# A decode layer on one core: the output transfer issued by SyncE behind the closing barrier instead of by ScalarE inside the block

## The chip, the core and the metric

The kernel runs on 1 core of one Trainium2 chip. The metric is the device time of one execution in microseconds (us). The kernel before takes 293.27 us (median of 3 runs, 293.23 to 293.54). Stamps in the text count from the span's start, the first instruction in the profile.

## What is computed

One decode step for two rows (B = 2, one token each): layer norm, attention over a sliding window of a cache, output projection, residual, layer norm, a gated feed-forward block, residual.

```python
W = min(4096, max(256, Sk // 4))          # 2048 of the 8192 cached positions
q = (x @ wq).reshape(B, Sq, Hq, Dh).transpose(0, 2, 1, 3)
k, v = k_cache[:, :, Sk - W:, :], v_cache[:, :, Sk - W:, :]
p = softmax(einsum("bhqd,bhkd->bhqk", q, k) * Dh ** -0.5)
a = einsum("bhqk,bhkd->bhqd", p, v).transpose(0, 2, 1, 3).reshape(B, Sq, Hq * Dh) @ wo

h  = x + A(layernorm(x))                  # A: the attention above
h2 = h + (gelu(n @ w_gate) * (n @ w_up)) @ w_down      # n = layernorm(h)
```

D = 640, 32 heads of 192, F = 1536, all in bfloat16. The output is [2, 1, 640], 2,560 bytes.

## The kernel before

Nearly everything is a stream of loads from HBM, 122.29 MB in all. A ring buffer in SBUF of six slots of 24,576 bytes per partition takes the keys and the values in 16 groups (two rows, four heads to a group), then the weights: wq after the first group of keys, wo in four parts, at the end w_gate, w_up in two pieces and w_down in four (`load`, `pump`, line 347). All loads are issued by SyncE, 44 of them, each when the slot that it overwrites has been read. TensorE transposes the keys (line 555), ScalarE and VectorE copy them out of PSUM, and scores, softmax and the product with the values follow group by group, in a loop of four trips on TensorE.

The program is written as a list of operations in order. `_Prog.op` notes for each the tiles that it reads (R) and writes (W) and the PSUM banks that it touches (X), and from these its dependences. `resolve` turns dependences into waits on semaphores, one for each engine's class of operations and one for each load. `emit` then puts one engine's operations into that engine's own stream, in the order of the list: waits, instruction, increment. Each engine has its own function inside `with nc.Block() as block` (lines 867 to 888). When the block closes, each engine branches out of its function, drains and enters a barrier: it increments one semaphore, GpSimd collects the increments and raises a second one, for which the others wait. In the profile all of this stands at line 867. Instructions written after the block come behind this barrier in the stream of the engine that has them. In the kernel before that is one wait on SyncE (line 890), for the semaphore `dout`.

The end of the computation, in the order of the code: the last two parts of the output projection (line 708), the sum of the hidden row and the second layer norm (lines 773 to 790), the products with w_gate and w_up (line 801) and the gate, with work on VectorE and ScalarE (the last operation on ScalarE is the activation at line 840, which scales the product with w_up), the transposes (line 810), the product with w_down in four pieces (line 850), the copy of the result from PSUM into the tile `yrow` on VectorE (line 856), and the transfer of `yrow` to the output in HBM (line 857), which ScalarE issues. It takes 8 rows of 160 elements, from every 16th partition of `yrow`, and writes them as [2, 4, 160]. ScalarE issues one other transfer, the load of x at the beginning (line 410).

A transfer adds 16 to its semaphore when it is complete. The waits on `dout` and on `yrow`'s writer are what orders the end:

```python
dve(lambda e: e.tensor_copy(yrow[0:113, :], m1[0:113, 0:160]), W=["y"], X=["m1"])
P.op("act", lambda e: e.dma_start(out..., yrow[0:113:16, :]), R=["y"], W=["out"], dma="dout")
...
nc.sync.wait_ge(sems["d", "dout"], 16)
```

Of the kernel before, what the change touches and what calls it, by code (L numbers as in the profile page):

```python
# [227 lines left out]
def bass_sequential_preLN__sliding_block_cached__geglu_ffn__decode_kernel(  # L228
# [12 lines left out]
    with ExitStack() as ctx:  # L241

        def sb(name, shape, dt):
            return ctx.enter_context(nc.sbuf_tensor(name, shape, dt))
# [66 lines left out]
        yrow = sb("yrow", [128, 160], BF16)  # L311
# [14 lines left out]
        P = _Prog()  # L326
# [62 lines left out]
        def dve(fn, R=(), W=(), X=(), cls=1):  # L389
            return P.op("dve", fn, R, W, X, cls=cls)  # L390
# [75 lines left out]
        def _x_T(e):  # L466
# [11 lines left out]
            R=["pi"] + [("bits", k) for k in range(11)], W=["pti"])  # L478
# [262 lines left out]
        for J in range(4):  # L741
# [32 lines left out]
           R=["rs", "bsel"], X=[("t", 3)])  # L774
# [47 lines left out]
        def rjb(t):  # L822
# [18 lines left out]
            W=[("osb", 0), ("osb", 1)], X=["o"])  # L841
        vT = ffn_columns(urow, [("osb", 0), ("osb", 1)], tps[1], 1)
        dve(tt(uT[:, :, 0:17:16].rearrange("p (r j) b -> p r j b", r=4), vT, rjb(ga[:, 0, :]), ALU.mult), R=["ga0"], W=["uT"], X=[("t", 1)])
        for i, (f0, f1) in enumerate(WDC):
            wd, wtoks = where["wd", i]

            def fn(e, f0=f0, f1=f1, wd=wd):
# [6 lines left out]

            pe(fn, R=["uT"] + wtoks, X=["m1"])
        dve(lambda e: e.tensor_copy(yrow[0:113, :], m1[0:113, 0:160]), W=["y"], X=["m1"])  # L856
        P.op("act", lambda e: e.dma_start(out[:, 0, :].rearrange("b (r n) -> r b n", r=4), yrow[0:113:16, :]), R=["y"], W=["out"],
             dma="dout")


        P.resolve({("dve", 0): 4 * 11, ("dve", 1): 8, ("act", 0): 4 * 6, ("pool", 0): 4})
        sems = {}
# [4 lines left out]
        with nc.Block() as block:  # L867

            @block.gpsimd
            def _(e):  # L870
                P.emit("pool", e, sems)

            @block.sync
            def _(e):
                P.emit("sp", e, sems)

            @block.vector
            def _(e):
                P.emit("dve", e, sems)

            @block.scalar
            def _(e):
                P.emit("act", e, sems)

            @block.tensor
            def _(e):
                P.emit_loop(e, sems, 4, ["a0", (0, None, ["oc"]), "a1", (0, 3, ["op"]), "a2", "b0", "b1", "b2", "c0", "c1", "c2",
                                         (None, 3, ["d0", "d1", "d2"])])

        nc.sync.wait_ge(sems["d", "dout"], 16)  # L890


# [26 lines left out]
```

## Time and profile before

| what | value |
|---|---|
| median of 3 runs | 293.27 us (293.23 to 293.54) |
| the profiled execution | 293.36 us |
| its span, first to last instruction | 291.9 us |
| mean granted TensorE clock | 0.849 |
| PE, matmuls | 197.7 us busy (68%) |
| PE, weight loads | 153.8 us (53%) |
| VectorE (DVE) | 128.4 us (44%) |
| ScalarE (ACT) | 96.2 us (33%) |
| GpSimd (POOL) | 8.6 us (3%) |
| queue of SyncE's loads (q1) | 6336 packets, 98.1% of the 16 DMA engines' span |
| queue of ScalarE's transfers (q10) | 16 packets, 0.0% |
| read from HBM | 122.29 MB, 419 GB/s over the span |

The span is shorter than the time of its own execution by 1.44 us (its unrounded value is 291.92): what lies ahead of the first and behind the last instruction of the program. An engine's share is busy time over the span; time in which a sequencer issues a transfer, waits, drains or takes part in a barrier is not counted as busy, and such instructions are named after their queue (ACTq, SPq). The chain that ended last is followed from the last compute instruction backwards; what lies behind that one (the output transfer, the barrier, the last wait) is not in it, and is read from the lines' own views. "Landing" is the last increment that a transfer makes on its semaphore.

### The profile page before, as it was taken

The numbers are of one execution on the slowest core, as the hardware profiler recorded it, in microseconds if no ns is written. First come the engines' busy times: TensorE is split into PE (matmuls) and PEld (weight loads), VectorE is DVE, ScalarE is ACT, GpSimd is POOL, SyncE is SP. The second block draws the span as 40 slices with busy tenths as digits, with TensorE's granted clock in tenths as the row PEclk, the third lists the DMA queues.
The fourth block names the chain that finished last, engine by engine and source line by source line (L and its number), as shares of the span: only waits on it lengthen the run. The fifth ranks groups of instructions, "written<-read, shape, count | busy, mean of one in ns | idle before, by whom it ended". The sixth has DMA issues, their size and how long they took to land.

```text
span 291.9 us, 5066 instructions
## 1 busy us (share of the span) xinstructions
PE 197.7 (68%) x2141; PEld 153.8 (53%) x2141; DVE 128.4 (44%) x311; ACT 96.2 (33%) x120; POOL 8.6 (3%) x36
## 2 busy tenths in 40 slices
PE   2570758858579197849594598658597858585784
PEld 1470445838376194629382585456575656563341
DVE  5960086434336254516264155426267426262231
ACT  2150125533333152616161154325254334251001
POOL 4000020000000000000000000000000000000000
PEclk9997799797959689987979589979689979796557
DMA  7997999999999999999999999999999999999994
GB/s 280 446 506 345 430 431 427 434 427 431 433 430 428 431 431 432 431 431 431 431 409 448 431 431 428 431 428 431 431 431 428 431 431 431 431 431 418 427 412 172
DMA packets 6362, 122.44 MB, mean 419 GB/s; under 512 B 718, under 2 KB 848, under 8 KB 1360
## 3 DMA queue, kind: packets, MB, share of 16 engines
q1 hardware_dynamic: 6336, 122.29, 98.1%
q8 instruction: 7, 0.11, 0.2%
q14 instruction: 3, 0.02, 0.0%
q10 hardware_dynamic: 16, 0.01, 0.0%
HBM read 122.29 MB, written 0.00 MB: 419 GB/s over the span
## 4 chain that ended last, share of the span: by engine, by line
DMA 76%; PE 20%; SPq 2%; DVE 1%; issue 0%
DMA ring<-in_A_k_cache_dram 57%; PE tps L555 16%; DMA ring<-in_A_wq_dram 10%; DMA ring<-in_B_w_down_dram 10%; SPq L347 2%; PE tps L576 2%; PE ops L657 1%; PE m L708 1%; PE m L690 1%; DVE ering L408 0%; PE m L641 0%; PE m L850 0%; DVE ktr L567 0%; PE m L671 0%; DVE yrow L856 0%
## 5 line engine op out<-in xcount | busy, mean ns | idle before, releaser
L555 PE MATMUL tps<-identf,ring 128*128 128x128 f32 x768 | 116.7, 322 | 46.8 <-DMA ring<-in_A_k_cache_dram 45.7
L555 PEld LDWEIGHTS tps<-identf,ring 128*128 128x128 f32 x768 | 107.9, 169 | 49.8 <-DMA ring<-in_A_k_cache_dram 47.1
L564 ACT ACTIVATE ktr<-tps 128x1024 bf16<-128x1024 bf16 x80 | 79.3, 1023 | 87.9 <-PE tps L555 87.9
L567 DVE COPY ktr<-tps 128x1024 bf16<-128x1024 bf16 x112 | 74.1, 688 | 74.9 <-PE tps L555 74.3
L632 ACT ACTIVATE eexp<-sm,nm 128x512 bf16<-128x512 f32 x16 | 11.5, 721 | 63.0 <-DVE nm L630 63.0
L657 PE MATMUL ops<-ring,ering 128*32 128x384 bf16 x512 | 25.0, 339 | 3.5 <-DMA ring<-in_A_v_cache_dram 3.4
L621 DVE CUSTOM_DVE_ANT_1 sm<-sps,mska 128x512 f32<-128x512 f32 x16 | 11.1, 691 | 33.7 <-PE sps L613 33.7
L613 PE MATMUL sps<-ktr,rq 128*16 128x512 bf16 x384 | 24.6, 388 | 1.1 <-POOL rq L408 1.1
L657 PEld LDWEIGHTS ops<-ring,ering 128*32 128x32 bf16 x512 | 12.7, 99 | 12.4 <-DMA ring<-in_A_v_cache_dram 5.4
L613 PEld LDWEIGHTS sps<-ktr,rq 128*16 128x16 bf16 x384 | 9.4, 88 | 11.3 <-POOL rq L408 1.2
L628 PEld LDWEIGHTS m<-mrhs,pm 128*128 128x128 bf16 x16 | 1.5, 96 | 23.4 <-DVE mrhs L404 23.4
L628 PE MATMUL m<-mrhs,pm 128*128 128x16 bf16 x16 | 2.9, 183 | 15.7 <-DVE mrhs L404 15.7
L408 POOL TENSOR_TENSOR rq<-qs,mask 128x96 bf16<-128x96 bf16 x16 | 5.6, 359 | 194.6 <-PE sps L613 161.4
L576 PE MATMUL tps<-ring,xnT 128*32 128x384 bf16 x80 | 5.0, 422 | 9.0 <-DMA ring<-in_A_wq_dram 9.0
L576 PEld LDWEIGHTS tps<-ring,xnT 128*32 128x32 bf16 x80 | 2.8, 121 | 11.0 <-issue 9.2
L408 DVE TENSOR_TENSOR ering<-m,mask 128x256 bf16<-128x256 f32 x16 | 6.7, 420 | 3.3 <-PE m L641 3.3
L599 DVE CAST qs<-ops 128x384 bf16<-128x384 f32 x1 | 0.6, 557 | 14.9 <-PE ops L594 14.9
L708 PE MATMUL m<-ring,ot 128*2 128x320 bf16 x96 | 5.5, 381 | 1.6 <-DMA ring<-in_A_wo_dram 1.6
L788 ACT ACTIVATE lnv<-tps,eps_t 98x1 f32<-98x1 f32 x1 | 0.3, 262 | 17.3 <-PE tps L786 17.3
L641 PE MATMUL m<-sel,eexp 128*128 128x64 bf16 x64 | 5.1, 207 | 1.2 <-ACT eexp L632 1.2
L641 PEld LDWEIGHTS m<-sel,eexp 128*128 128x128 bf16 x64 | 4.8, 112 | 1.7 <-DVE nm L630 1.3
L408 DVE TENSOR_TENSOR orow<-m,wm 128x1536 bf16<-128x1536 f32 x3 | 5.3, 1751 | 0.0
(124 smaller groups left out, 84.7 us busy)
## 6 DMA issues: line engine op xcount, KB each, us to landing
ring<-in_A_k_cache_dram SPq DMA_DIRECT2D x16, 3072.0 KB, 31.7
ring<-in_A_v_cache_dram SPq DMA_DIRECT2D x16, 3072.0 KB, 27.6
ring<-in_A_wq_dram SPq DMA_DIRECT2D x1, 7680.0 KB, 28.2
ring<-in_A_wo_dram SPq DMA_DIRECT2D x4, 1920.0 KB, 21.7
ring<-in_B_w_gate_dram SPq DMA_DIRECT2D x1, 1920.0 KB, 32.4
ring<-in_B_w_up_dram SPq DMA_DIRECT2D x1, 1536.0 KB, 24.7
ring<-in_B_w_down_dram SPq DMA_DIRECT2D x1, 960.0 KB, 27.2
ring<-in_B_w_down_dram SPq DMA_DIRECT2D x1, 480.0 KB, 27.9
```

Of the source, the lines that this page charges most:

```text
L347: P.op("sp", lambda e, v=v, src=src: e.dma_start(v, src), W=toks + [("sem", sem)], dma=sem)
L408: return lambda e: e.tensor_tensor(out=out, in0=a, in1=b, op=op)
L555: ins = e.transpose(tps[bi][:, 128 * u:128 * (u + 1)], kv[:, off:off + 128], identf[:, :])
L564: act(lambda e, dst=dst, bv=bv: e.activation(out=dst, in_=bv, func=ACT.Copy), W=[("kt", n)], X=[("t", bi)])
L567: dve(lambda e, dst=dst, bv=bv: e.tensor_copy(dst, bv), W=[("kt", n)], X=[("t", bi)], cls=0)
L576: ins = e.matmul(tps[0][32 * r:32 * (r + 1), 0:384], lhsT=xnT[:, c, 32 * J:32 * (J + 1)], rhs=wq[:, c, 1536 * J + 384 * r:1536 * J + 384 * ...
L613: ins = e.matmul(sps[32 * ch:32 * ch + 16, :], lhsT=rq[:, g % 4, k, :], rhs=ktr[:, k // 2, 1024 * ch + k % 2:1024 * (ch + 1):2], start=(k ...
L621: dve(lambda e: e.tensor_tensor_reduce(out=sm[:, :].rearrange("p (u x) -> p u x", u=4), in0=sps[:, :].rearrange("p (u x) -> p u x", u=4), ...
L632: act(lambda e: e.activation(out=eexp[:, :], in_=sm[:, :], func=ACT.Exp, bias=nm[:, 0:1], scale=1.0, accum_out=zr[:, g % 4:g % 4 + 1]), R= ...
L641: ins = e.matmul(o, lhsT=eexp[:, 128 * u:128 * (u + 1)], rhs=sel64[:, :], start=True, stop=True)
L657: ins = e.matmul(ops_[32 * r:32 * (r + 1), 0:384], lhsT=ering[:, g % 4, t, :], rhs=vv[:, 384 * t:384 * (t + 1)], start=(g % 4 == 0 and t < 4),
L708: ins = e.matmul(m1[32 * r:32 * r + 2, 192:512], lhsT=ot[:, kk, :], rhs=wo[:, kk - k0, 320 * h:320 * (h + 1)], start=(kk == 1 or J < 2 and ...
```

## The change

The transfer of `yrow` is listed as an operation of SyncE instead of ScalarE and its handle is kept as `last`. SyncE's function in the block emits all of SyncE's operations but this one; it is emitted after the block, ahead of the wait for `dout`. Its dependence on the copy into `yrow` stays, as a wait on VectorE's semaphore in front of it. Source, destination and semaphore are the same. In the streams: ScalarE has one instruction less at its end; SyncE has one more between the closing barrier and its last wait; PE, VectorE and GpSimd have the same instructions in the same order.

```diff
         dve(lambda e: e.tensor_copy(yrow[0:113, :], m1[0:113, 0:160]), W=["y"], X=["m1"])
-        P.op("act", lambda e: e.dma_start(out[:, 0, :].rearrange("b (r n) -> r b n", r=4), yrow[0:113:16, :]), R=["y"], W=["out"],
-             dma="dout")
+        last = P.op("sp", lambda e: e.dma_start(out[:, 0, :].rearrange("b (r n) -> r b n", r=4), yrow[0:113:16, :]), R=["y"], W=["out"],
+                    dma="dout")
...
             @block.sync
             def _(e):
-                P.emit("sp", e, sems)
+                P.emit("sp", e, sems, [o for o in P.per["sp"] if o is not last])
...
+        P.emit("sp", nc.sync, sems, [last])
         nc.sync.wait_ge(sems["d", "dout"], 16)
```

## The prediction

> **What bounds the kernel now.** I read the page first (the load on the DMA engines and the chain that ended last), then that chain in order of time at its end, then the closing barrier's own line, then who waited on SyncE, and last the DMA engines over the final 2.4 us.
>
> ```profile
> DMA  7997999999999999999999999999999999999994
> ...
> DMA 76%; PE 20%; SPq 2%; DVE 1%; issue 0%
> ```
>
> The kernel is a stream of loads: the 16 DMA engines are 90% busy or more in nearly all slices, and 76% of the chain is loads. Nothing in the change touches a load, so the first 289 us are left as they are. Only the end is in question: the window of the timeline and of the chain behind the last load.
>
> ```profile
> 260.82 28.19 DMA ring<-in_B_w_down_dram
> 289.01 0.04 issue
> 289.05 0.74 PE m L850 x12
> 289.79 0.02 issue
> 289.81 0.33 DVE yrow L856
> ...
> 290.17 0.64 ACTq L857 DMA_DIRECT2D out_dram<-yrow  x1
> ```
>
> The last piece of w_down lands, 12 matmuls run, VectorE writes yrow (289.815 to 290.140 in the trace's stamps), and ScalarE issues the output transfer at 290.174, 34 ns later. The span ends at 291.92, so 1.74 us lie between that issue and the end. Next, the barrier (line 867, its columns: engine, operation, duration in ns, start) and the two waits on SyncE:
>
> ```profile
> L867 POOLq EVENT_SEMAPHORE  x2: 17/17/17, 291.4 to 291.5; - x2
> ...
> L867 SPq DRAIN  x1: 129/129/129, 265.5 to 265.5; - x1
> L867 PEldq DRAIN  x1: 370/370/370, 289.5 to 289.5; - x1
> L867 DVEq DRAIN  x1: 364/364/364, 289.8 to 289.8; - x1
> L867 ACTq DRAIN  x1: 485/485/485, 290.9 to 290.9; - x1
> L867 SPq EVENT_SEMAPHORE  x1: 17/17/17, 291.5 to 291.5; - x1
> ...
> SPq L867 <- PEq L867: 25.9, 1, 25.9
> SPq L904 <- PEq L904: 0.7, 1, 0.7
> SPq L890 <- DMA out_dram<-yrow: 0.4, 1, 0.4
> ```
>
> ScalarE reaches the barrier last: its DRAIN ends at 291.343, after all others (VectorE's ends at 290.194). GpSimd collects at 291.374, releases at 291.453, SyncE is through at 291.494. Then SyncE still waits 0.4 us for the output to land (its last record is at 291.901). So the transfer sets the end, and the barrier is hidden under it with 0.4 us to spare. (SyncE's wait is put down to PEq; the stamps show that it was ScalarE's DRAIN.) When the 12 packets of the transfer moved is in the DMA view over 289.5 to 291.9 us, 0.06 us a slice:
>
> ```profile
> GB/s 0 0 0 0 0 0 0 0 0 0 0 0 0 0 0 0 0 0 0 0 0 0 0 0 0 0 0 0 0 0 0 0 16 27 0 0 0 0 0 0
> ```
>
> Only slices 33 and 34 have bytes: first packet at 291.458, last one over at 291.557. So the 1.74 us split as 0.64 issue, 0.64 from its end to the first packet, 0.10 packets, 0.33 to the last semaphore increment (291.884), 0.03 to the end.
>
> **The change part by part.** (a) ScalarE loses one DMA issue and with it the long DRAIN behind it. Its last work is then the activation at line 840, over at 286.29, so ScalarE reaches the barrier early, and VectorE becomes the last to arrive: its increment stands at 290.204. This takes 1.15 us off the barrier (291.350 to 290.204), which by itself is worth nothing, since the barrier is hidden now; it sets when SyncE may go on.
>
> (b) SyncE's issue now stands behind the barrier. What follows the last increment is read from the barrier of before: 24 ns to GpSimd's collecting, 103 ns to its release, 144 ns to SyncE's record, and 82 ns from such a record to a following DMA issue (the barrier at the start: SyncE's record at 0.654, its first issue at 0.736; ScalarE shows 78 ns). 144 + 82 = 226 ns. The issue starts at 290.204 + 0.226 = 290.430 instead of 290.174: 0.256 us later. Nothing is queued behind it on SyncE but the final wait; the 44 load issues stand before it and were over at 265.457, and the last load had landed at 289.41, so its queue is empty. The wait for yrow that it carries is fulfilled before the barrier opens and costs nothing of its own. If the barrier were late for another reason, the issue would be late by as much; PE's increment is at 289.838, which leaves 0.37 us of cover.
>
> (c) The issue and the way to the first packet, on SyncE instead of ScalarE. No row of before has this shape on SyncE. The nearest:
>
> ```profile
> L347 SPq DMA_DIRECT2D ring<-in_A_k_cache_dram x16: 534/604/930, 0.7 to 219.1; - x16
> ...
> L347 SPq DMA_DIRECT2D ring<-in_A_wo_dram x4: 334/384/592, 74.2 to 247.1; - x4
> ...
> L410 ACTq DMA_DIRECT2D xrow<-in_A_x_dram x1: 554/554/554, 0.7 to 0.7; - x1
> ```
>
> Lower bound: the shortest issue of the wo kind, 0.334, plus the way to the first packet of the small x load on ScalarE (issue over at 1.291, packet at 1.691: 0.40) gives 0.73 us, against 1.284 for the output on ScalarE: 0.55 less. Upper bound: the first K load after the barrier at the start, 0.632 for the issue and 0.777 to its packet, and 0.10 more for a shape in two dimensions that also writes 12 of 16 increments itself (an estimate: the 0.644 of the output on ScalarE less the 0.535 of a K issue that had waited): 1.51, which is 0.23 more. I take the same 1.284 us as on ScalarE, because in the barrier at the start both engines took like times for their first simple issues (0.566 for wq on SyncE, 0.554 for x on ScalarE): 0.0.
>
> (d) Packets, landing and the final wait: 0.443 us from first packet to SyncE's last record, kept; the destination is the same and the DMA engines are idle in both.
>
> Trainium skill, "DMA: Bandwidth & Descriptors", section on the anatomy of one DMA: it puts most of a fixed cost of about 2 us into the receipt of the write, which would leave (c) next to nothing to vary. The trace differs: 0.33 us from the last packet to the increment, 1.28 before the first packet. By the page the sum would be 0.256 us with hardly any spread; the rows leave it open by -0.55 to +0.23.
>
> Sum: 0.256 + 0 + 0 = +0.26 us on the path. The profiled execution had a span of 291.92 and a run time of 293.36, that is 0.09 over the median of 293.27 and inside the runs shown (293.23 to 293.54). The 1.44 us around the span follow SyncE's last record and are kept: the increments of a semaphore that the program doesn't own go on at 292.04, 0.12 us after that record, after two at 291.80 and 291.83. New span 292.18, profiled run 293.62, and from the median **293.53 us**, +0.09%.
>
> **The rivals.**
>
> 1. SyncE's way to the DMA engines is shorter. For it: behind the output's issue ScalarE's twelve own increments show only at 291.235, 0.42 us after the issue's end, where x's showed 0.08 us after; and SyncE's DRAIN took 0.129 us against 0.485 on ScalarE. If that 0.34 us is ScalarE's alone, the sum is 0.26 - 0.34 = -0.08: 293.19. At the lower bound, 0.26 - 0.55 = -0.29: 292.98. Against: x was issued on the same engine with no delay, so it may well belong to the shape, which moves along.
>
> 2. Other side, slower: SyncE stands at the barrier for 25 us and then must get new code for the rest of its program, because the issue now lies behind the branch that ends the block. Fetches show as packets of the instruction queues, 16 KB taking 0.99 to 1.11 us and 8 KB 0.31 to 0.53. One exposed 16 KB fetch costs about 1.0 us: 0.26 + 1.0, that is 294.5. It decides as soon as more than about 0.33 us of it is exposed, since 0.26 is spent already. Against: SyncE's DRAIN, which stands behind that branch too, began at 265.515, 58 ns after the last issue, so the code was there, and the 25 us of waiting leave time for more. The Trainium skill, "Runtime: NRT & Kernel Launch", section on instruction fetch, says that a taken branch out of the two fetched pages stalls for a fetch; by that rule 294.5, and the trace shows no such stall at this branch.
>
> 3. Faster by more than the bound: the four other engines leave the barrier 1.15 us earlier (290.35 instead of 291.50) and do their share of the 1.44 us behind the program while the output is under way. If the whole 1.15 us came off the path, the time would be 293.53 - 1.15 = 292.38; it counts as faster from 0.85 us on (0.59 and the 0.26 to be made up). Against: the increments quoted above go on only after SyncE's last record, so the closing is serial behind it, and SyncE is the last engine in both kernels.
>
> 4. The change doesn't do what it says: the issue is put before the barrier after all and only changes engine. Then it starts at 290.17 as now and the time is 293.27. The order of instructions has it behind the barrier's release, so this is nearly excluded.
>
> **How the numbers follow.** A run here is told from no change at about 0.2%, 0.59 us. Forecast (0 to +0.5 us): 0.61, within the bound. Rival 1 (-0.3 to 0): 0.17, within it. Rival 2: 0.14, slower. Rival 3: 0.07, faster. Rival 4: 0.01, within it. That is 0.07 faster, 0.79 within, 0.14 slower. The likeliest one's time is 293.53. The range takes in both bounds of (c), 292.98 and 293.27 + 0.26 + 0.23 = 293.76, with 0.14 more on top for the spread of the runs: 292.98 to 293.90. It leaves out rivals 2 and 3.
>
> **What would show it.** Right: ScalarE's DRAIN moves to about 286.3 and is short; VectorE's becomes the last at the barrier; SyncE's barrier record stands near 290.35 and its issue at 290.43 (shifted with the end of yrow); the issue takes 0.55 to 0.70 us, first packet 1.28 us after its start, final record 0.44 us after that; SyncE's last wait grows from 0.4 us to over 1 us. Wrong: more than 0.1 us between barrier record and issue, with an instruction fetch in it (rival 2); a first packet less than 1.0 us after the issue's start (rival 1); a run time that falls while the span grows (rival 3); or a change in the loads before 289 us, for which I have no cause.

## The result and the profile after

The change makes the kernel slower: 294.30 us (median of 7 runs, 294.11 to 294.50) against 293.31 us (7 runs, 293.23 to 293.54) for the kernel before. The ratio is 1.0034, with a 95% interval from 1.0024 to 1.0044, that is 0.99 us and beyond the 0.2% that a run can tell from no change. The profiled execution took 294.44 us, its span is 293.0 us.

The loads are not the cause. The chain of the kernel after, at its end and in order of time, is the old one within 0.05 us, and the output's issue follows it (first the chain, then the line from the timeline):

```profile
260.84 28.22 DMA ring<-in_B_w_down_dram
289.06 0.04 issue
289.10 0.74 PE m L850 x11
289.84 0.02 issue
289.86 0.33 DVE yrow L856
...
290.47 0.69 SPq L857 DMA_DIRECT2D out_dram<-yrow  x1
```

The barrier's line and who waited on SyncE:

```profile
L867 SPq DRAIN  x1: 123/123/123, 265.6 to 265.6; - x1
L867 ACTq DRAIN  x1: 611/611/611, 285.7 to 285.7; - x1
L867 PEldq DRAIN  x1: 372/372/372, 289.5 to 289.5; - x1
L867 DVEq DRAIN  x1: 364/364/364, 289.9 to 289.9; - x1
L867 SPq EVENT_SEMAPHORE  x1: 17/17/17, 290.4 to 290.4; - x1
...
SPq L867 <- PEq L867: 24.7, 1, 24.7
SPq L891 <- DMA out_dram<-yrow: 1.8, 1, 1.8
```

VectorE is now the last at the barrier, SyncE is through it at 290.394 and issues at 290.473. So far all is as the steps had it. But the wait for the output, 0.4 us before, is 1.8 us. The DMA engines from 289.5 to 293.1 us, 0.09 us a slice, show why; first the kernel before, then the kernel after, each with the queues that moved something:

```profile
GB/s 0 0 0 0 0 0 0 0 0 0 0 0 0 0 0 0 0 0 0 0 0 11 18 0 0 0 0 0 0 0 0 0 0 0 0 91 0 0 0 0
...
q14 instruction: 1, 0.01, 0.9%
q10 hardware_dynamic: 12, 0.00, 0.3%
```

```profile
GB/s 0 0 0 0 0 0 0 0 0 0 0 0 0 0 0 0 0 0 0 0 0 0 0 91 0 21 0 7 0 0 0 0 0 0 0 0 0 0 0 0
...
q14 instruction: 1, 0.01, 0.6%
q1 hardware_dynamic: 12, 0.00, 0.3%
```

Stamps of single packets and increments, here and below, are from the trace's records, not from a view. The slice with 91 GB/s is one packet of 8,192 bytes on an instruction queue: an engine fetches its next code (the runs below show that it is VectorE). Before, it stood at 292.70, behind the output's packets and behind the end of the span. After, it stands at 291.60, ahead of them, and the output's packets fall into two parts (slices 25 and 27): nine at 291.765 to 291.823, and the last three at 291.956 to 291.989. Those three carry two of the eight rows and one of the four increments, and they start as the fetch's packet ends (291.960). The four increments come at 292.171, 292.178, 292.184 and, 0.76 us behind, at 292.946. SyncE's last record is at 292.962. (The transfer's packets ended at 291.998, so the last increment comes 0.95 us after the last packet, where it was 0.33 before.)

From the end of yrow to SyncE's last record it was 1.76 us and is 2.77 us. The 1.01 us more are 0.25 for the later issue, 0.01 for the way from the issue's start to the first packet (1.292 against 1.284) and 0.75 behind the first packet. Times from the end of yrow are what the experiments are compared by; the ends of the span differ by some 0.1 us between executions of one kernel.

### The profile page after: what moved, and what is told of

It reads as the page before. It is cut to its first block, busy times and chain, and to the rows that moved or that the text cites. A ratio compares the mean times of both kernels' runs of the same rounds, so it can differ in the third digit from the quotient of the medians.

```text
span 293.0 us, 5066 instructions
## 1 busy us (share of the span) xinstructions
PE 191.8 (65%) x2141; PEld 148.4 (51%) x2141; DVE 128.2 (44%) x311; ACT 96.1 (33%) x120; POOL 8.6 (3%) x36
## 4 chain that ended last, share of the span: by engine, by line
DMA 77%; PE 18%; SPq 2%; DVE 1%; ACT 1%; issue 0%
DMA ring<-in_A_k_cache_dram 57%; PE tps L555 14%; DMA ring<-in_B_w_down_dram 10%; DMA ring<-in_A_wq_dram 10%; PE tps L576 2%; SPq L347 2%; PE ops L657 1%; DVE ktr L567 1%; ACT ktr L564 1%; PE m L708 1%; PE m L690 1%; DVE ering L408 0%; PE m L850 0%; PE m L671 0%; DVE yrow L856 0%
## 5 line engine op out<-in xcount | busy, mean ns | idle before, releaser
L555 PE MATMUL tps<-identf,ring 128*128 128x128 f32 x768 | 112.1, 313 | 48.7 <-DMA ring<-in_A_k_cache_dram 47.5
L555 PEld LDWEIGHTS tps<-identf,ring 128*128 128x128 f32 x768 | 103.4, 164 | 52.1 <-DMA ring<-in_A_k_cache_dram 48.9
L708 PE MATMUL m<-ring,ot 128*2 128x320 bf16 x96 | 4.3, 318 | 2.5 <-DMA ring<-in_A_wo_dram 2.5
L583 ACT ACTIVATE qrow<-tps 128x768 bf16<-128x768 f32 x1 | 0.8, 811 | 14.6 <-PE tps L576 14.6
```

Source lines behind the costliest of these rows:

```text
L555: ins = e.transpose(tps[bi][:, 128 * u:128 * (u + 1)], kv[:, off:off + 128], identf[:, :])
L708: ins = e.matmul(m1[32 * r:32 * r + 2, 192:512], lhsT=ot[:, kk, :], rhs=wo[:, kk - k0, 320 * h:320 * (h + 1)], start=(kk == 1 or J < 2 and ...
```

## The experiments

**Is it SyncE, or the place behind the barrier?** Theory A: the fetch of another engine, which the early barrier sets off, holds the output back. Theory B: SyncE's queue lands a store late.

```diff
# sp_inside, against the change: SyncE issues inside the block
-                P.emit("sp", e, sems, [o for o in P.per["sp"] if o is not last])
+                P.emit("sp", e, sems)
-        P.emit("sp", nc.sync, sems, [last])
```

> The transfer is issued by SyncE as in the change, but inside the block, ahead of the barrier. Theory A (an 8 KB instruction fetch, which starts 1.2 us after the barrier's release, shares a DMA engine with the output): the issue starts 0.03 us after yrow, the barrier is held by SyncE's DRAIN until about 291.35, the output lands about 1.75 us after the issue's start, before the fetch at about 292.6; span 291.9 to 292.0, time 293.3. Theory B (a store on SyncE's queue, behind 44 loads, completes late whatever the barrier does): one increment comes 0.76 us after the others again; span 292.7, time 294.0 to 294.1.

Measured: 293.43 us against 293.37, ratio 0.9999 (0.9989 to 1.0009), no difference. The issue took 0.690 us, SyncE's DRAIN held the barrier until 291.43, all four increments came together (291.912 to 291.967), and the fetch at 292.82. SyncE's last wait is 0.4 us, as before. SyncE's queue is not late.

```profile
SPq L890 <- DMA out_dram<-yrow: 0.4, 1, 0.4
```

```diff
# act_behind, against the change: ScalarE issues behind the barrier
-        last = P.op("sp", ...
+        last = P.op("act", ...
-        P.emit("sp", nc.sync, sems, [last])
+        P.emit("act", nc.scalar, sems, [last])
```

> The transfer stays with ScalarE, but is issued behind the barrier. Theory A: the release stands at 290.4 as in the change, the fetch at 291.6, and the output's packets meet it; one of four increments 0.7 to 0.8 us after the others; SyncE's last record at 292.9, time 294.2 to 294.4. Theory B: ScalarE's queue lands as before, 0.26 to 0.3 us later; last record at 292.2, time 293.6.

Measured: 294.43 us against 293.37, ratio 1.0034 (1.0022 to 1.0047), the change's whole loss with the old issuer. The fetch stood at 291.934, three increments at 292.172 to 292.185, the fourth at 293.280. SyncE's last wait, which here begins at the barrier:

```profile
SPq L891 <- DMA out_dram<-yrow: 2.9, 1, 2.9
```

The fetch came 0.3 us later than expected (1.51 us behind VectorE's barrier record, 1.20 in the change); why, these runs do not show. The place costs it, not the engine, and Theory B falls.

**Does it go when no engine runs ahead, and whose fetch is it?**

```diff
# all_wait, behind the last line of the change; pe_wait, dve_wait, act_wait, pool_wait: one of these lines each
         nc.sync.wait_ge(sems["d", "dout"], 16)
+        nc.tensor.wait_ge(sems["d", "dout"], 16)
+        nc.vector.wait_ge(sems["d", "dout"], 16)
+        nc.scalar.wait_ge(sems["d", "dout"], 16)
+        nc.gpsimd.wait_ge(sems["d", "dout"], 16)
```

> The change, and PE, VectorE, ScalarE and GpSimd also wait for the output's semaphore behind the barrier, so that no engine can go on and fetch before the output has landed. Theory A: no packet of an instruction queue between 290.4 and the landing; all four increments together at about 292.18, SyncE's last record at 292.2, span 292.2 to 292.3. The time does not fall by the whole 0.76 us, since what the engines do behind the barrier begins at 292.2 and not at 291.5 as before: 293.36 + 0.7, about 294.0. Theory B: the last increment stays at 292.9, span 293.0, time 294.4 or more.

Measured: 294.12 us against 293.37, ratio 1.0025 (1.0015 to 1.0035). The clash is gone: four increments together at 292.036 to 292.085, SyncE's last record at 292.101, the fetch at 293.246. The time keeps most of the loss, as expected: time less span is 1.91 us on the mean here and 1.46 in the runs of the kernel before beside it, since now every engine starts what it does behind the program only when the output has landed.

> The change, and of the other engines PE alone also waits for the output's semaphore behind the barrier. Theory: one engine's fetch meets the output, so in exactly one of these four runs the instruction packet moves behind the landing, the four increments come together and SyncE's last record stands 1.75 us after the issue's start (time about 294.0); in the other three one increment is 0.7 to 1.1 us late (last record 2.5 to 2.8 us after the issue's start, time 294.2 to 294.5). PE has a 16 KB fetch of its own kind in the loop, so its fetch would show on another queue: I expect no effect here. Rival: any engine's going on is enough, then none of the four helps.

> The same with VectorE alone waiting. VectorE has the most instructions after PE and so the likeliest 8 KB fetches (three before the end in the trace): I expect the instruction packet to move behind the landing here, last record 1.75 us after the issue's start, time about 294.0. If it is not VectorE's, one increment stays 0.7 to 1.1 us late and the time is 294.2 to 294.5.

> The same with ScalarE alone waiting. Not its fetch: one increment 0.7 to 1.1 us late, time 294.2 to 294.5. Its fetch: all four together, about 294.0.

> The same with GpSimd alone waiting. Not its fetch: one increment 0.7 to 1.1 us late, time 294.2 to 294.5. Its fetch: all four together, about 294.0.

One run each, the kernel before at 293.24 beside them: 294.52 (PE), 293.88 (VectorE), 294.27 (ScalarE), 294.70 (GpSimd). SyncE's wait for the output, with PE, VectorE, ScalarE and GpSimd waiting too in turn; it is 1.8 us in the change:

```profile
SPq L891 <- DMA out_dram<-yrow: 1.8, 1, 1.8
```

```profile
SPq L891 <- DMA out_dram<-yrow: 1.0, 1, 1.0
```

```profile
SPq L891 <- DMA out_dram<-yrow: 1.8, 1, 1.8
```

```profile
SPq L891 <- DMA out_dram<-yrow: 1.8, 1, 1.8
```

Exactly one engine ends it, in one run each: VectorE. (The times of PE's and GpSimd's runs lie above the 294.2 to 294.5 that were expected, but not at the end that is looked at here: time less span is 1.6 and 1.8 us there, 1.44 in the kernel before beside them.) In VectorE's run the output's packets stay together and the fetch follows the landing (289.5 to 293.1 us; the fetch is the last slice):

```profile
GB/s 0 0 0 0 0 0 0 0 0 0 0 0 0 0 0 0 0 0 0 0 0 0 25 4 0 0 0 0 0 0 0 0 0 0 0 0 0 0 0 91
```

From the end of yrow to SyncE's last record it is 2.02 us there, 0.26 more than before: what the prediction had. The other 0.4 us of its 0.64 lie behind the span, which fits that VectorE leaves the program at 291.98 with the landing and not at 291.53 with the barrier as before.

**Can the fetch be moved instead of waited for?** VectorE's stream gets 32 instructions that do nothing, early, while it idles (at 18.6 to 21.9 us, ahead of the copy into `qs`, the place that `pad_at` notes), so that its last page of code is due sooner.

```diff
# dve_pad, against the change; before_pad: the same against the kernel before
-                P.emit("dve", e, sems)
+                P.emit("dve", e, sems, P.per["dve"][:pad_at[0]])
+                for _ in range(64):
+                    e.wait_ge(sems["pool", 0], 1)
+                P.emit("dve", e, sems, P.per["dve"][pad_at[0]:])
```

> The change, with 64 waits that are already fulfilled (32 instructions) put into VectorE's stream while it idles before the queries are ready, so that its stream reaches the next 8 KB of code before the end. No wait is added at the end. Theory A (VectorE's fetch holds one increment back): no instruction packet after 289 us, the four increments together, last record 1.75 us after the issue's start, span 292.2, time 293.5 to 293.65, that is the change without its clash. If the fetch is bound to the barrier's release and not to the place in the stream, it stays 1.2 us after the release, and the time is 294.3.

> Control for the padding: the kernel before with the same 64 fulfilled waits on VectorE. Its fetch came after the output had landed, so Theory A expects no difference: 293.2 to 293.5. A gain of 0.3 us or more would say that the padding does something else than move a fetch out of the output's way.

Measured: 294.37 us for the padded change (294.31 to 294.50) and 294.30 us for the padded kernel before (294.21 to 294.33), the kernel before without padding at 293.32. Both numbers miss what was expected, because the padding has a price of its own, 0.98 us: the last fetch moved to 247.5 us, into the stream of loads, and in the padded kernel before, TensorE waited 4.2 us for the last group of keys where it waited 3.2. The increments of the loads show why. A load has 16 of them. In the padded kernel before, the last one comes 0.21 to 0.24 us behind the next to last for the loads that land between 180 us and the fetch, and 1.12 to 1.24 us behind it for every load that lands after it; without padding it is 0.26 to 0.30 all the while. The last piece of w_down has 15 increments by 289.187 (289.141 without padding) and the last at 290.333 (289.407), and the end of yrow moves with it, by 0.92 us. So this fetch, too, holds back one of the parts of a transfer, and here that part stays late to the end; that it is the fetch is inferred from the time, since its 247.5 us lie where the gap jumps, in both padded kernels (0.23 to 1.19 and 0.22 to 1.21).

The end, which the run was made for, is clean. DMA engines of the padded change from 289.95 to 293.15 us, 0.08 us a slice, and its wait for the output:

```profile
GB/s 0 0 0 0 0 0 0 0 0 0 0 0 0 0 0 0 0 0 0 0 0 0 0 0 0 0 0 0 0 0 0 0 0 0 28 4 0 0 0 0
...
q1 hardware_dynamic: 12, 0.00, 0.4%
...
SPq L896 <- DMA out_dram<-yrow: 1.0, 1, 1.0
```

No instruction queue, and increments at 293.069 to 293.127. From the end of yrow to the last record it is 2.02 us against 1.76 in the padded kernel before, and the medians of the two padded kernels are 0.07 us apart. So without the clash the same change costs 0.26 us on the path and about a tenth of a microsecond in the time, since some 0.13 us come back behind the span (time less span is 1.32 us on the mean in the padded change and 1.45 in the padded kernel before); the fetch belongs to a place in VectorE's stream, not to the barrier as such.

**What is held: the packets, or the increment?** SyncE is made to wait between barrier and issue, by fulfilled waits.

```diff
# delay: 24 waits; delay_short: 10
+        for _ in range(24):
+            nc.sync.wait_ge(sems["pool", 0], 1)
         P.emit("sp", nc.sync, sems, [last])
```

> The change, with 24 fulfilled waits (12 instructions, some 0.3 to 0.6 us) on SyncE between barrier and issue. Theory A, the increment waits for the fetch to be written: in the four runs with a clash whose fetch I have read, the last increment stands 1.345 us after the fetch's start whatever its own packets did. So the delay costs nothing: last increment still 1.35 us after the fetch's start, about 292.95, time 294.3. Theory B, the output's own packets are what is late: they now come after the fetch and are not held, but everything is later by the delay: all four together at 292.5 to 292.8, time 293.9 to 294.1. If the last increment stays 0.7 us behind the others, the time is 294.6 to 294.9.

Measured: 294.22 us (294.13 to 294.31), no slower than the change's 294.30. But the delay came out at 0.74 us, counted from the end of yrow, more than meant, and the last increment is due at 292.94 by either theory (it came at 292.943, the other three at 292.859 to 292.883), so it only shows that 0.7 us of delay are free.

> The change with 10 fulfilled waits (5 instructions of 60 ns, so 0.30 us) on SyncE between barrier and issue. The longer delay came out 0.72 us and could not tell the two theories apart, since both end at 292.94 with it. Here the output's packets come at about 292.07, after the fetch has left its DMA engine (about 291.95). Theory A, the increment waits until the fetch is written: three increments 1.70 us after the issue's start (292.47), the fourth 1.345 us after the fetch's start (292.94 where that start is 291.60), time 294.2 to 294.4, the delay free. Theory B, only packets that stand behind the fetch on the DMA engine are late: all four by 292.5, time 293.85 to 294.0, faster than the change although it issues later.

Measured: 294.24 us (294.19 to 294.69) against 293.30. DMA engines from 289.5 to 293.1 us and the wait:

```profile
GB/s 0 0 0 0 0 0 0 0 0 0 0 0 0 0 0 0 0 0 0 0 0 0 91 0 0 0 0 0 21 7 0 0 0 0 0 0 0 0 0 0
...
SPq L893 <- DMA out_dram<-yrow: 1.5, 1, 1.5
```

The fetch is off its DMA engine at 291.962, and all packets come after it (292.040 to 292.196). Three increments are in time at 292.467 to 292.480, the fourth comes at 292.910. Theory B had all four by 292.5 and falls. So it isn't the place in the queue alone: the increment itself waits. For what, shows in its distance from the fetch's start:

| run | issue's start | fetch's start | last increment | behind the fetch's start |
|---|---|---|---|---|
| the change | 290.473 | 291.600 | 292.946 | 1.346 |
| act_behind | 290.500 | 291.934 | 293.280 | 1.346 |
| pe_wait | 290.384 | 291.516 | 292.861 | 1.345 |
| act_wait | 290.227 | 291.361 | 292.756 | 1.395 |
| pool_wait | 290.328 | 291.464 | 292.808 | 1.344 |
| delay_short | 290.753 | 291.563 | 292.910 | 1.347 |

In five of the six runs it is the same to 3 ns, and 0.05 longer where the fetch's packet took longest (0.572 us). The issue's start is from 0.81 to 1.43 us ahead of the fetch and doesn't matter here. The Trainium skill, "DMA: Bandwidth & Descriptors", section on queues, rings and completion order, says that a completion increment lands only after every earlier write of its DMA engine, across its queues. The trace agrees, with 1.345 us as the time until the fetch no longer holds it; that the two stood on the same DMA engine is inferred, since the records don't name the engine. Why it is 1.345 us, when the fetch's own packet is over after 0.31 to 0.57, no run here shows.

**Is there a version that beats both?** The kernel before, with the output cut in two transfers, each with its own semaphore; SyncE's last wait is for both.

```diff
# split, against the kernel before (first halves of the lines)
+        P.op("act", lambda e: e.dma_start(out[0, 0, :].rearrange("(r n) -> r n", r=4), yrow[0:97:32, :]), ...
+        P.op("sp", lambda e: e.dma_start(out[1, 0, :].rearrange("(r n) -> r n", r=4), yrow[16:113:32, :]), ...
```

> A version that might beat both: the kernel before with the output as two transfers of 4 rows in one dimension, row 0 from ScalarE and row 1 from SyncE, both inside the block. Issues in one dimension took 0.33 to 0.55 us in the trace against 0.64 to 0.69 for this output. If issue and way to the first packet shorten by 0.1 to 0.2 us, both landings and the barrier move by as much: 293.1 to 293.25. If not: 293.3 to 293.4.

Measured: 293.57 us against 293.32, ratio 1.0008 (0.9998 to 1.0018): no gain, and the median lies above both expectations. The two issues took nearly as long as the one (0.612 us on ScalarE against 0.644, 0.662 on SyncE against 0.690), though each has one dimension and half the rows, and both DRAINs grew (0.485 on ScalarE in the kernel before, 0.423 on SyncE in sp_inside):

```profile
L867 ACTq DRAIN  x1: 670/670/670, 290.9 to 290.9; - x1
L867 SPq DRAIN  x1: 687/687/687, 290.9 to 290.9; - x1
...
L857 ACTq DMA_DIRECT2D out_dram<-yrow x1: 612/612/612, 290.2 to 290.2; - x1
...
L858 SPq DMA_DIRECT2D out_dram<-yrow x1: 662/662/662, 290.2 to 290.2; - x1
```

## Why the prediction was wrong, step by step

(a) Right. ScalarE's DRAIN moved to 285.7 (0.611 us, the activation at line 840 included), VectorE's became the last, and the barrier opened 1.10 us earlier (290.394 against 291.494), or 1.15 counted from the end of yrow, as forecast.

(b) Right. The issue was forecast 0.256 us later and came 0.25 us later, counted from the end of yrow. The 226 ns that the old barrier gave from the last increment to an issue were 222.

(c) Right. The value taken was the 1.284 us of ScalarE; SyncE needed 1.292, as 0.690 of issue and 0.602 to the first packet. The section of the Trainium skill that the prediction set beside this step ("DMA: Bandwidth & Descriptors", anatomy of one DMA) describes transfers that GpSimd issues. This one came from ScalarE and SyncE, so the difference that the prediction found says nothing against that section.

(d) This step failed: "0.443 us from first packet to SyncE's last record, kept; the destination is the same and the DMA engines are idle in both." It was 1.197 us. The destination is the same, but the DMA engines were not idle: moving the barrier's release by 1.1 us moved VectorE's fetch by 1.1 us, from 292.70 to 291.60, into the output's way. What had been late enough to be harmless was a packet of the trace of before, behind the span's end, and I had read its kind (8 KB on an instruction queue) only for SyncE. With 1.197 in the place of 0.443, the sum of 0.26 becomes 1.01 on the path; the time grew by 0.99.

Rival 1 (a shorter way on SyncE) is out: SyncE's own increments, too, showed late, 0.38 us behind the issue's end against ScalarE's 0.42, so that the delay belongs to this transfer and not to ScalarE. So does the long DRAIN: behind the output SyncE's took 0.423 us in sp_inside, not 0.129.

Rival 2 named an instruction fetch, but of the wrong engine and with another effect: a stall of SyncE ahead of its issue. SyncE's issue stood 0.079 us behind its barrier record, without a fetch; the fetch that did harm was VectorE's, and it held an increment. The rival's time of 294.5 came near by chance, and the rule of the Trainium skill that was set beside it did not decide here.

Rival 3 saw that the other engines leave early, and asked only what they would gain by it. They did leave early; one of them did harm. Its argument against rests on a misreading: the increment at 292.04, and one at 292.09 behind it, were not set off by SyncE's last record. They belong to other engines, 0.59 and 0.63 us behind the barrier's release at 291.453. In the change four such increments stand at 290.697 to 290.988, as far behind the release at 290.353 (0.34 to 0.64 us, 0.34 to 0.63 before). So the closing is not wholly behind SyncE's last record, and the 1.44 us around the span are not quite kept: on the mean, time less span is 1.30 to 1.34 us in the five kernels with the issue behind the barrier and no wait added at the end, and 1.43 to 1.48 in the kernels with it inside the block. The gain exists, and is about a tenth of a microsecond, not 1.15.

The range had its upper end, 293.90, from the bounds of (c) and 0.14 for the spread of the runs. Step (d) had been given no bounds, though a transfer that moves in time by a quarter of a microsecond, beside engines that move by one, can meet other traffic.

## What to carry to other kernels

A barrier at the end also decides when the other engines go on, and with that when they fetch code. Before a last transfer is put behind one, read the packets of the instruction queues around the end, those behind the span too, and move them by as much as the barrier moves. A completion increment can wait for a stranger's write: look at the increments one by one. Here one of four was late where the fetch was in the way, and all four moved together where the issue was delayed past it (the longer delay).

## What the runs showed that I had not expected

- A fetch of 8,192 bytes, whose packet takes 0.3 to 0.6 us, held an increment until about 1.345 us after its start, even where the transfer's packets came after it.
- The issue of the output took 0.61 to 0.65 us on ScalarE and 0.66 to 0.69 on SyncE, in one dimension or two, for 4 rows or 8. Of SyncE's 44 loads in the kernel before, 42 took 0.33 to 0.63, one 0.93 and one 4.16.
- Fulfilled waits on SyncE stand two to an instruction, and such an instruction costs about 60 ns (24 waits came to 0.74 us); these 0.74 us were free here.
- 32 idle instructions on an idle engine cost 0.98 us in the whole: they moved a fetch of 8,192 bytes into the stream of loads, and from then on one of the 16 increments of every load came about 1 us later against the others.
